# Top-k attention with a mixture of experts: split up products in the tail, small work and idle transposes elsewhere in the first steps

## The chip, the core and the metric

The kernel runs on one core of one Trainium2 chip. The engines are TensorE (PE in the profile; PEld its weight loads), VectorE (DVE), ScalarE (ACT), GpSimd (POOL) and SyncE (SP, which here issues DMAs). The metric is the device time of one execution in microseconds; less is better. "Clock" is TensorE's granted clock as a share of 2.4 GHz, so 0.50 is 1.2 GHz.

## What is computed

```python
# q, k, v: (8, 8, 576, 64); top_k = 32; 4608 tokens, D = 512, 8 experts, F = 1024
scores = scale * np.matmul(q, k.transpose(0, 1, 3, 2))
kth = np.partition(scores, -top_k, axis=-1)[..., -top_k:-top_k + 1]
scores = np.where(scores >= kth, scores, -1000000000.0)
attn = np.exp(scores - scores.max(-1, keepdims=True))
attn = attn / (attn.sum(-1, keepdims=True) + 1e-09)
x = (attn @ v).transpose(0, 2, 1, 3).reshape(B * S, H * D)
logits = x @ w_gate
e_idx = np.argmax(logits, axis=1)
...
for e in range(E):
    mask = e_idx == e
    h = np.maximum(x[mask] @ w1[e], 0.0)
    out[mask] = gate_w[mask, None] * eom[mask, e, None] * (h @ w2[e])
```

## The kernel before, in words

Rows of queries come in 36 tiles of 128; a step handles two heads of one tile, so there are 144 steps (`NSTEP`), and four steps make a tile. In step i DVE finds the largest scores of step i in three rounds (`rank`: L308 MAX, L311 MATCH_REPLACE), ACT then marks what lies below the 24th (`below`, L335), POOL adds marks and scores (L338), DVE takes the next eight from that sum (`window`, L350), reads the scores of the step after (`gmax`, L301), picks the 32nd value of step i-1 (`choose`: L361 twice, in the first steps also L365) and multiplies that step's exponentials by the mask (`weigh`, L377). In the first steps, i < `LONE` = 48 and not `exact`, called `calm`, the second head is masked on another way: `choose` leaves the negated value (L365), ACT marks with it (`veil`, L384), POOL adds (L387), and ACT takes the exponential (`unveil`, L393). PE computes scores (L274), transposes the weighted exponentials (`flip`, L404), and on even steps multiplies by v (`attend`, L436). On odd calm steps, where there is no `attend`, it transposes the identity 12 times into a bank that nobody reads (the idle transposes, L910).

What is done per finished tile and per group of tiles (sums and reciprocals L501 and L502, gates, routing L520 to L566, tables of slots) waits in queues and is issued one operation at a time by `fill(n)`. Its calls stood between the rounds of `rank` (three of one), before and after `choose` (one each) and at the end of the step (three). PE's part of it (`side_start`, "side work") goes beside the transposes of a step.

Tokens are routed in groups; each group gives expert slots of 128 tokens with one expert each, 40 in all. A slot loads w1 and w2 of its expert (2 MB each, L670 and L677 on SP's queue), gathers its rows (`fetch_x`, POOL), transposes them (`turn`), multiplies by w1 (`up_products`, L714, 128x128 pieces in plain f32), rectifies, multiplies by w2 (`down`) and scatters (`put`, L740). 25 slots are done inside the steps. The other 15, called the tail and numbered 25 to 39 here, follow after the last step in `slots_in_turn`: there w2 is split into two factors of type f32r, a rounded part (ACT, L1015) and the rest (DVE, L1016), the rectified result likewise (L1023, L1024), and the down product is three products of 128x512 for each of eight pieces (L1033). Buffers: two each of w1t and w2t, so a load waits until the readers of the buffer two slots back are done. Each engine takes its instructions in the order in which the program issues them. The table of the last slots (`slot_table(..., True)`, 25 small DVE operations) is issued by `background` during the first tail slot.

Of the kernel before, what the change touches and what calls it, by code (L numbers as in the profile page):

```python
# [23 lines left out]
P = 128  # L24
# [15 lines left out]
def tile_topk_attention_moe(  # L40
# [143 lines left out]
    def run(exact, stack):  # L184
# [688 lines left out]
        for i in range(NSTEP + 4):  # L873
            t, hp = divmod(i, NHP)
            step[0] = i
            if i + 1 < NSTEP and (i + 1, 0) not in SC:
                scores(i + 1)()
            for r in range(3):
                if i < NSTEP:
                    rank(i, r)  # L880
                    if r == 0:
                        shift(i)
                fill(1)
# [6 lines left out]


            calm = i < LONE and not exact
            mid = None
# [52 lines left out]
            fill(1)  # L946
            if 1 <= i <= NSTEP:
                choose(i - 1)
                fill(1)
# [8 lines left out]
            fill(3)  # L958
# [40 lines left out]
        def slots_in_turn():  # L999

            def prepare(n):
                ahead("id", fetch_id, n + 2)
                ahead("x", fetch_x, n + 1)
                ahead("w1", fetch_w1, n)
                ahead("w2", fetch_w2, n)

            def turned(n):
                ahead("turn", lambda s, *_: turn(s, pools["p"], "pm")(), min(n, had["x"] - cur[0]))

            def split(s, part):  # L1010

                w = W[s][1][:, 4 * part:4 * part + 4]
                hi, lo = [pools["w"].tile([P, 4, DM], F32R, name=n, bufs=3) for n in ("w2h", "w2l")]
                HL[s, part] = hi, lo
                nc.scalar.activation(hi, w, AF.Copy)  # L1015
                nc.vector.tensor_tensor(lo, w, hi.bitcast(F32), op=ALU.subtract)  # L1016

            def up_split(s, f0):
                if f0 == 0:
                    HT[s] = [pools["w"].tile([P, NF, P], F32R, name=n, bufs=1) for n in ("hth", "htl")]  # L1020
# [5 lines left out]
            def down_split(s, f0):  # L1026
                if f0 == 0:
                    PY[s] = pools["p"].tile([P, DM], F32, name="pm")
                hh, hl = HT[s]
                wh, wl = HL.pop((s, f0 // 4))  # L1030
                for f in range(f0, f0 + 4):
                    for k, (h, w) in enumerate(((hh, wh), (hh, wl), (hl, wh))):
                        nc.tensor.matmul(PY[s], h[:, f, :], w[:, f - f0, :], start=(f == 0 and k == 0),  # L1033
                                         stop=(f == NF - 1 and k == 2))

            def splitted(s, part):
                if s < min(len(order), had["w2"]) and (s, part) not in HL:
                    split(s, part)
            while cur[0] < len(order):
                s = cur[0]  # L1040
                prepare(1)
                turned(1)
                prepare(2)
                splitted(s, 0)
                splitted(s, 1)
                ahead("w2", fetch_w2, 3)
                for f0 in (0, 4):
                    up_split(s, f0)
                    yield
                ahead("w1", fetch_w1, 3)  # L1050
                turned(2)
                for part in range(2):
                    splitted(s + 1, part)
                    down_split(s, 4 * part)
                    yield
                put(s)
                cur[0] += 1
# [8 lines left out]
        background()  # L1066
        for _ in slots_in_turn():
# [77 lines left out]
```

## Time and profile before

| | us |
|---|---|
| median of 3 runs (1290.36 to 1293.07) | 1291.58 |
| profiled execution, time | 1289.37 |
| profiled execution, span from first to last instruction | 1287.5 |
| PE busy | 1185.5 (92%) |
| DVE busy | 1136.0 (88%) |
| ACT busy | 981.1 (76%) |
| POOL busy | 755.9 (59%) |

Busy shares are means over stretches with different limits: the calm steps take up the first 340 us or so, the other steps run to about 1060 us, the tail from 1080 to 1276 us. What a change is worth is read in its own stretch. Durations of PE's records overlap, so the distance between starts is the better measure there.

### The profile page before, as it was taken

To read this page: it belongs to the slowest core of one execution; us is meant where nothing else is said; L and a number is where in the kernel's file an instruction comes from. 1 tells how busy PE (TensorE), PEld (TensorE's weight loads), DVE (VectorE), ACT (ScalarE), POOL (GpSimd) and SP (SyncE) were. 2 spreads that over 40 slices of the span, in tenths; PEclk is the share of its full clock that TensorE was granted. 3 is DMA by queue.
4 is the path that set the end of the run, shared out by engine and by line. 5 is a ranking of instruction groups with operands and counts; after the bars stand their busy time and mean duration, and the time that the engine had idled before them with its cause. 6 is when DMAs were issued, how large, how long until landed. Compare 5 with 4: busy or idle time off the path is not lost.

```text
span 1287.5 us, 31729 instructions
## 1 busy us (share of the span) xinstructions
PE 1185.5 (92%) x10084; PEld 918.3 (71%) x10084; DVE 1136.0 (88%) x6112; ACT 981.1 (76%) x1928; POOL 755.9 (59%) x1221
## 2 busy tenths in 40 slices
PE   6777777777799999999999999999999999999996
PEld 4554655655577777777777777777777777999995
DVE  7999999999999999999999999999999954544443
ACT  6999999899888888878888888888878854454542
POOL 6666666698775766756767666567656733212110
PEclk7989899899899999999999999999999999999998
DMA  5400210201827663765465565755554468999980
GB/s 136 76 17 18 71 54 18 55 18 55 295 79 228 208 224 107 252 226 157 171 202 162 203 220 151 273 208 182 181 173 149 165 228 295 386 366 337 364 336 21
DMA packets 109384, 227.49 MB, mean 177 GB/s; under 512 B 14858, under 2 KB 33546, under 8 KB 108176
## 3 DMA queue, kind: packets, MB, share of 16 engines
q1 hardware_dynamic: 99536, 205.67, 47.6%
q0 software_dynamic: 7552, 18.96, 4.3%
q8 instruction: 83, 1.36, 0.5%
q10 hardware_dynamic: 2112, 0.68, 0.3%
q14 instruction: 101, 0.83, 0.2%
HBM read 206.68 MB, written 20.69 MB: 177 GB/s over the span
## 4 chain that ended last, share of the span: by engine, by line
PE 57%; DVE 26%; issue 14%; POOL 3%; ACT 1%; POOLq 0%; ACTq 0%
PE pm L714 14%; PE pm L729 13%; PE po L436 9%; PE ps L274 9%; PE pst L404 8%; DVE cand L301 8%; DVE v L350 5%; DVE cand L311 3%; DVE ep L377 3%; DVE v L308 3%; DVE x L361 2%; PE pst L457 1%; POOL xg L693 1%; PE pst L703 1%; POOL out_dram L740 1%
## 5 line engine op out<-in xcount | busy, mean ns | idle before, releaser
L338 POOL TENSOR_TENSOR w<-s,marks 128x576 f32<-128x576 f32 x288 | 362.8, 1281 | 191.0 <-ACT marks L335 184.5
L301 DVE MAX8 cand<-s 128x8 f32<-128x72 f32 x2304 | 322.0, 218 | 8.0 <-ACT s L282 8.0
L714 PE MATMUL pm<-xs,w1t 128*128 128x128 f32 x2560 | 296.8, 276 | 0.9 <-ACT xs L706 0.8
L714 PEld LDWEIGHTS pm<-xs,w1t 128*128 128x128 f32 x2560 | 292.0, 192 | 2.4 <-ACT xs L706 1.1
L404 PE MATMUL pst<-ident,ep 128*128 128x128 f32 x1296 | 210.6, 291 | 66.0 <-ACT ep L393 60.9
L404 PEld LDWEIGHTS pst<-ident,ep 128*128 128x128 f32 x1296 | 152.0, 146 | 152.2 <-ACT ep L393 68.7
L335 ACT ACTIVATE marks<-s,v 128x576 int8<-128x576 f32 x288 | 220.8, 770 | 40.8 <-DVE v L308 38.9
L350 DVE MAX8 v<-w 128x8 f32<-128x576 f32 x288 | 202.2, 744 | 0.0
L412 ACT ACTIVATE pT<-pst 128x512 f32<-128x512 f32 (+1 forms) x432 | 197.9, 481 | 5.5 <-PE pst L404 4.2
L282 ACT ACTIVATE s<-ps 128x1152 f32<-128x1152 f32 (+1 forms) x145 | 162.5, 1121 | 50.0 <-PE ps L274 49.9
L274 PE MATMUL ps<-kst,qst 64*128 64x288 f32 (+1 forms) x1280 | 189.7, 448 | 5.4 <-ACT s L282 5.4
L377 DVE SCALAR_TENSOR_TENSOR ep<-s,kth,ep 128x576 f32<-128x576 f32 x240 | 188.4, 814 | 0.3 <-issue 0.3
L436 PE MATMUL po<-pT,v 128*64 128x128 f32 (+3 forms) x3200 | 188.6, 270 | 0.0
L436 PEld LDWEIGHTS po<-pT,v 128*64 128x64 f32 (+1 forms) x3200 | 160.6, 139 | 34.4 <-issue 32.8
L729 PE MATMUL pm<-w2t,ht 128*128 128x512 f32 x400 | 180.4, 594 | 0.0
L345 ACT ACTIVATE ep<-s,v 128x576 f32<-128x576 f32 x240 | 175.5, 778 | 0.0
L740 POOL DMA_INDIRECT out_dram<-y,idt x40 | 49.9, 1247 | 189.5 <-ACT y L736 173.2
L308 DVE MAX8 v<-cand 128x8 f32<-128x64 f32 x864 | 147.7, 213 | 0.0
L274 PEld LDWEIGHTS ps<-kst,qst 64*128 64x128 f32 (+1 forms) x1280 | 101.6, 184 | 46.2 <-issue 18.2
L729 PEld LDWEIGHTS pm<-w2t,ht 128*128 128x128 f32 x400 | 72.4, 191 | 72.3 <-issue 72.3
L311 DVE MATCH_REPLACE8 cand<-v,cand 128x64 f32<-128x64 f32 x576 | 116.1, 209 | 0.0
L1016 DVE TENSOR_TENSOR w2l<-w2t,w2h 128x2048 fp32r<-128x2048 f32 x30 | 67.9, 2290 | 29.8 <-ACT w2h L1015 29.8
(165 smaller groups left out, 1434.8 us busy)
## 6 DMA issues: line engine op xcount, KB each, us to landing
w1t<-in_w_dram SPq DMA_DIRECT2D x40, 2048.0 KB, 9.4
w2t<-in_w_dram SPq DMA_DIRECT2D x40, 2048.0 KB, 11.7
v<-in_va_dram SPq DMA_DIRECT2D x8, 1152.0 KB, 6.8
x_rows<-xu SPq DMA_DIRECT2D x36, 256.0 KB, 2.1
qst<-in_qa_dram SPq DMA_DIRECT2D x70, 128.0 KB, 10.8
kst<-in_ka_dram SPq DMA_DIRECT2D x14, 576.0 KB, 8.1
ids<-far SPq DMA_DIRECT2D x1, 678.0 KB, 10.8
xg<-x_rows,idt POOLq DMA_INDIRECT x40, 7.0
```

Of the source, the lines that this page charges most:

```text
L274: nc.tensor.matmul(ps[qs, a, n, :288], Q[t][rows, hp, qs], K[b][rows, hp, cols], start=True, stop=True)
L301: nc.vector.max(out=c[:, 8 * g:8 * g + 8], in_=SC[i, a][:, g * GW:(g + 1) * GW])
L308: nc.vector.max(out=vs[:, a, 8 * r:8 * r + 8], in_=cs[a])
L335: nc.scalar.activation(m.bitcast(I8).rearrange("p (s b) -> p s b", b=2)[:, :, 1], s, AF.Sign, bias=vs[:, a, PIVOT - 1:PIVOT], scale=-(1.0 ...
L338: nc.gpsimd.tensor_tensor(w, s, m, op=ALU.add)
L350: nc.vector.max(out=VV[i][0][:, a, 24:32], in_=SW[i][0][a])
L377: nc.vector.scalar_tensor_tensor(e, SC.pop((i, a)), kth_col(i, a), e, op0=ALU.is_ge, op1=ALU.mult, accum_out=SM[t][:, 2 * hp + a:2 * hp + ...
L404: nc.tensor.transpose(ps[:, c - c0, :], pt[:, c * P:(c + 1) * P], ident)
L412: nc.scalar.activation(x, ps[:, :n, :], AF.Copy)
L436: nc.tensor.matmul(po[a * 64:(a + 1) * 64, k, qs], lhs, rhs, start=half and not k and not m, stop=(c == 3 and k == 1 and m == len(TT[t]) - 1))
L714: nc.tensor.matmul(ph[:, f - f0, :], w[:, c, f * P:(f + 1) * P], XS[s][:, c, :], start=(c == 0), stop=(c == NC - 1))
L729: nc.tensor.matmul(PY[s], HT[s][:, f, :], w[:, f, :], start=(f == 0), stop=(f == NF - 1))
```

## The change

In calm steps `fill` is no longer called between the rounds of `rank` nor before `choose`; it issues up to four between `choose` and `weigh` and up to four at the end. On steps with neither `attend` nor side work beside the transposes, 24 idle transposes stand for 12. In the tail x and w1 are split as w2 was, the up product becomes 12 products of 128x512 for each half of F with x as the stationary side, and its rectified result, which now has tokens on partitions, is transposed by PE (`turn_half`) before it is split. The slots overlap: the down product of slot s-1 stands after the up product of slot s. The first tail slot keeps the plain up product (`up_plain`). The last table is issued before the first tail slot where nothing else is pending.

```diff
@@ the loop over steps
+            calm = i < LONE and not exact
             for r in range(3):
                 if i < NSTEP:
                     rank(i, r)
...
-                fill(1)
+                if not calm:
+                    fill(1)
...
-                for c in range(12):
+                for c in range(12 if beside else 24):
                     nc.tensor.transpose(idle[:, c % 4, :], ident, ident)
...
-            fill(1)
+            if not calm:
+                fill(1)
             if 1 <= i <= NSTEP:
                 choose(i - 1)
-                fill(1)
+                fill(4 if calm else 1)
                 weigh(i - 1)
...
-            fill(3)
+            fill(4 if calm else 3)
@@ slots_in_turn
+            def parted(x, hi, lo):
+                nc.scalar.activation(hi, x, AF.Copy)
+                nc.vector.tensor_tensor(lo, x, hi.bitcast(F32), op=ALU.subtract)
+            def splitted(s, m, half):
+                if s < min(len(order), had["w2" if m else "w1"]) and (s, m, half) not in HL:
+                    w = W[s][m][:, 4 * half:4 * half + 4] if m else W[s][m][:, :, 512 * half:512 * half + 512]
+                    HL[s, m, half] = parts([P, 4, 512], (("w1h", "w1l"), ("w2h", "w2l"))[m])
+                    parted(w, *HL[s, m, half])
+            def products(ps, x, c0, w, first, last):
+                for c in range(4):
+                    for k, (a, b) in enumerate(((0, 0), (0, 1), (1, 0))):
+                        nc.tensor.matmul(ps, x[a][:, c0 + c, :], w[b][:, c, :], start=(first and c == 0 and k == 0),
+                                         stop=(last and c == 3 and k == 2))
+            def up_half(s, half):
+                ph = pools["p"].tile([P, 512], F32, name="pm")
+                products(ph, XS[s], 0, HL.pop((s, 0, half)), True, True)
+                HS[half] = pools["w"].tile([P, 4, P], F32, name="hs")
+                nc.scalar.activation(HS[half].rearrange("p c q -> p (c q)"), ph, AF.Relu)
+            def turn_half(s, half):
...
+                for c in range(4):
+                    nc.tensor.transpose(pt[:, c, :], HS[half][:, c, :], ident)
+                parted(pt, *[x[:, 4 * half:4 * half + 4, :] for x in HT[s]])
...
+                    up_half(s, 0)
                     yield
+                    splitted(s + 1, 0, 0)
+                    up_half(s, 1)
+                    yield
+                    turned(2)
+                    splitted(s + 1, 0, 1)
+                if done is not None:
+                    down_half(done, 0)
+                    yield
+                if s is not None:
+                    splitted(s, 1, 0)
+                    turn_half(s, 0)
+                    turn_half(s, 1)
+                if done is not None:
+                    down_half(done, 1)
+                    put(done)
+                    yield
+                if s is not None:
+                    splitted(s, 1, 1)
@@ ahead of the tail
+        if not (urgent or small or side):
+            small_end()
+            small_end = None
+            background()
```

Three places in the order of instructions. The first is DVE in a calm step in which the sums of a finished tile are inverted (r is the reciprocal, v the values found, x the choice, ep the weighted exponentials); before:

```order
L377 SCALAR_TENSOR_TENSOR ep,sums<-s,kth,ep 128x576
L308 MAX v_1618<-cand 128x8 x2
L311 MATCH_REPLACE cand<-v_1618,cand 128x64 x2
L501 TENSOR_SCALAR r<-sums 128x8
L308 MAX v_1618<-cand 128x8 x2
L311 MATCH_REPLACE cand<-v_1618,cand 128x64 x2
L502 RECIPROCAL r<-r 128x8
L308 MAX v_1618<-cand 128x8 x2
```

and after:

```order
L350 MAX v_1571<-w 128x8 x2
L301 MAX cand<-s 128x8 x16
L361 SCALAR_TENSOR_TENSOR x_1803,kth<-left,n,v_1571 128x8
L361 SCALAR_TENSOR_TENSOR x_1805,kth<-left,n,v_1571 128x8
L365 TENSOR_SCALAR less<-kth 128x1
L501 TENSOR_SCALAR r<-sums 128x8
L502 RECIPROCAL r<-r 128x8
L377 SCALAR_TENSOR_TENSOR ep,sums<-s,kth,ep 128x576
```

L501 and L502 moved from the rounds of `rank`, behind the weighing, to between `choose` and the next weighing. The second is ACT at the start of the tail (y of slot 24, then x of slot 25); before:

```order
L736 ACTIVATE y<-pm,idt 128x512
L706 ACTIVATE xs<-pm 128x512
L1015 ACTIVATE w2h<-w2t 128x2048 x2
L1023 ACTIVATE hth<-pm 128x512 x2
L706 ACTIVATE xs<-pm 128x512
L1015 ACTIVATE w2h<-w2t 128x2048 x2
```

and after, where w1h and w2h are the rounded parts, hth and hs the rectified results of slots 25 and 26:

```order
L706 ACTIVATE xs<-pm 128x512
L1008 ACTIVATE w1h<-w1t 128x2048
L1066 ACTIVATE hth<-pm 128x512
L1008 ACTIVATE xsh<-pm 128x512
L1008 ACTIVATE w1h<-w1t 128x2048
L1066 ACTIVATE hth<-pm 128x512
L1008 ACTIVATE w2h<-w2t 128x2048 x2
L1045 ACTIVATE hs<-pm 128x512
L1008 ACTIVATE w1h<-w1t 128x2048
L1045 ACTIVATE hs<-pm 128x512
```

A split of w1 of slot 27 now stands on ACT between the two rectifying copies of slot 26. The third is PE in step 3, an odd calm step; before:

```order
L404 MATMUL pst<-ident,ep 128x128 x8
L910 MATMUL pm<-ident 128x128 x12
L404 MATMUL pst<-ident,ep 128x128
L274 MATMUL ps<-kst,qst 128x288 x4
```

and after:

```order
L404 MATMUL pst<-ident,ep 128x128 x8
L911 MATMUL pm<-ident 128x128 x24
L404 MATMUL pst<-ident,ep 128x128
L274 MATMUL ps<-kst,qst 128x288 x4
```

Only the number of idle transposes changed, here and on twelve more steps.

## Rows read from the trace of the kernel before

**Rows 1.** Stretches: length, busy time (count) by engine, clock, DMA share, GB/s.

```profile
core 0: us, PE busy (x) PEld busy (x) DVE busy (x) ACT busy (x) POOL busy (x), PEclk, DMA share, GB/s
0.00:340.00 340.00, 255.50 (x2319) 189.67 (x2319) 329.87 (x1984) 300.32 (x635) 234.66 (x346) 0.91 0.24 65
1080.00:1276.00 196.00, 195.58 (x1376) 180.86 (x1376) 95.03 (x94) 90.35 (x89) 36.88 (x43) 1.00 0.86 318
```

**Rows 2.** Timeline of calm steps: start, duration, engine, line, operation, [idle before, releaser].

```profile
105.57 0.81 DVE L377 SCALAR_TENSOR_TENSOR ep<-s,kth,ep 128x576 f32<-128x576 f32 x1
106.67 1.27 POOL L387 TENSOR_TENSOR w<-s,marks 128x576 f32<-128x576 f32 x1 [1.41 <-ACT marks L384]
106.97 1.01 DVE L501 TENSOR_SCALAR r<-sums 128x8 f32<-128x8 f32 x1
...
112.81 0.81 DVE L377 SCALAR_TENSOR_TENSOR ep<-s,kth,ep 128x576 f32<-128x576 f32 x1
...
119.05 0.81 DVE L377 SCALAR_TENSOR_TENSOR ep<-s,kth,ep 128x576 f32<-128x576 f32 x1
```

**Rows 3.** L501 to 340 us: group (busy us, mean ns), line (min/median/max ns).

```profile
L501 DVE TENSOR_SCALAR r<-sums 128x8 f32<-128x8 f32 x11 | 8.4, 760 | 0.0
...
L501 DVE TENSOR_SCALAR r<-sums x11: 160/1014/1077, 52.9 to 327.4; 128x8 f32<-128x8 f32 x11
```

**Rows 4.** Timeline of PE in two calm steps.

```profile
44.29 0.33 PE L404 MATMUL pst<-ident,ep 128*128 128x128 f32 x1 [2.37 <-ACT ep L393]
...
120.62 1.48 PE L910 MATMUL pm<-ident 128*128 128x128 f32 x12
124.94 0.47 PE L404 MATMUL pst<-ident,ep 128*128 128x128 f32 x1 [2.85 <-ACT ep L393]
```

**Rows 5.** Stretches right behind those two waits, columns as in rows 1.

```profile
44.00:48.00 4.00, 3.71 (x37) 2.71 (x39) 3.96 (x29) 3.62 (x8) 2.43 (x4) 1.00 0.86 297
125.00:128.00 3.00, 3.00 (x20) 1.45 (x21) 2.96 (x24) 1.90 (x4) 1.60 (x3) 0.50 0.00 0
```

**Rows 6.** Timeline of DVE, line L361 (`choose`) in calm steps.

```profile
77.63 1.01 DVE L361 SCALAR_TENSOR_TENSOR x<-left,n,v 128x8 f32<-128x8 f32 x1
78.56 0.22 DVE L361 SCALAR_TENSOR_TENSOR x<-left,n,v 128x8 f32<-128x8 f32 x1
...
131.69 0.91 DVE L361 SCALAR_TENSOR_TENSOR x<-left,n,v 128x8 f32<-128x8 f32 x1
...
213.37 0.97 DVE L361 SCALAR_TENSOR_TENSOR x<-left,n,v 128x8 f32<-128x8 f32 x1
```

**Rows 7.** Timeline of PE in the tail.

```profile
1093.58 7.30 PE L714 MATMUL pm<-xs,w1t 128*128 128x128 f32 x64
...
1100.72 0.60 PE L703 MATMUL pm<-ident,xg 128*128 128x128 f32 x4
1101.08 0.48 PE L1033 MATMUL pm<-w2h,hth 128*128 128x512 f32 x1
...
1237.39 7.31 PE L714 MATMUL pm<-xs,w1t 128*128 128x128 f32 x64
...
1250.46 7.31 PE L714 MATMUL pm<-xs,w1t 128*128 128x128 f32 x64
```

**Rows 8.** Groups in the tail (busy us, mean ns), and one row of ACT's timeline.

```profile
L1016 DVE TENSOR_TENSOR w2l<-w2t,w2h 128x2048 fp32r<-128x2048 f32 x30 | 67.9, 2290 | 29.8 <-ACT w2h L1015 29.8
L1015 ACT ACTIVATE w2h<-w2t 128x2048 fp32r<-128x2048 f32 x30 | 57.3, 1918 | 5.8 <-PE pm L1033 4.2 <-DMA w2t<-in_w_dram 1.6
...
1231.66 0.60 ACT L1023 ACTIVATE hth<-pm 128x512 fp32r<-128x512 f32 x1 [2.98 <-PE pm L714]
```

**Rows 9.** A stretch of the tail, columns as in rows 1.

```profile
1100.00:1120.00 20.00, 20.00 (x131) 18.04 (x131) 9.69 (x7) 10.97 (x11) 2.57 (x3) 1.00 1.04 392
```

**Rows 10.** Loads of w1t, slots 26 (first line) and 27: landing, issue on SP.

```profile
DMA to landing us min/median/max: 9.4/9.4/9.4
...
1087.86 0.37 SPq L670 DMA_DIRECT2D w1t<-in_w_dram  x1
...
DMA to landing us min/median/max: 15.1/15.1/15.1
```

More of the change, by code (lines that the diff above doesn't have):

```diff
@@ L889, in run @@
             early, late, last = [], [], []
-            calm = i < LONE and not exact
-            mid = None
+            mid, beside = None, None
             if calm and 2 <= i:
@@ L999, in slots_in_turn @@
         def slots_in_turn():
[L1001 to L1005, printed above, removed]
-            def turned(n):
[L1008 to L1016, printed above, removed]
@@ new lines, in turned @@
+            def turned(n):
+                ahead("turn", lambda s, *_: turn_split(s), min(n, had["x"] - cur[0]))
+                for s in range(cur[0], had["turn"]):
+                    if not isinstance(XS[s], list):
+                        x = XS[s]
+                        XS[s] = parts([P, NC, P], ("xsh", "xsl"))
+                        parted(x, *XS[s])
+            def splitted(s, m, half):
[3 more added lines that the diff above has]
+                    parted(w, *HL[s, m, half])
@@ L1019, in up_split, with up_plain @@
+            def up_plain(s, f0):
                 if f0 == 0:
-                    HT[s] = [pools["w"].tile([P, NF, P], F32R, name=n, bufs=1) for n in ("hth", "htl")]
+                    HT[s] = parts([P, NF, P], ("hth", "htl"))
                 ph = up_products(s, f0)
@@ L1024, in up_split @@
                 nc.vector.scalar_tensor_tensor(lo, ph, 0.0, hi.bitcast(F32), op0=ALU.max, op1=ALU.subtract)
[L1026 to L1048, printed above, removed]
-                    yield
[L1050 to L1054, printed above, removed]
-                    yield
-                put(s)
-                cur[0] += 1
+            if cur[0] == len(order):
+                return
@@ new lines, in slots_in_turn @@
+            done = cur[0]
+            ahead("id", fetch_id, 3)
+            ahead("w1", fetch_w1, 2)
+            ahead("w2", fetch_w2, 2)
+            if had["turn"] == done:
+                ahead("x", fetch_x, 2)
+                ahead("turn", lambda s, *_: turn(s, pools["p"], "pm")(), 1)
+            ahead("x", fetch_x, 3)
+            cur[0] += 1
+            for half in range(2):
+                splitted(done + 1, 0, half)
+                up_plain(done, 4 * half)
+                if not half:
+                    turned(1)
+                yield
@@ new lines, in slots_in_turn @@
+            ahead("w1", fetch_w1, 2)
+            splitted(done, 1, 0)
+            splitted(done, 1, 1)
+            while cur[0] < len(order) or done is not None:
+                s = cur[0] if cur[0] < len(order) else None
+                if s is not None:
+                    ahead("id", fetch_id, 3)
+                    ahead("x", fetch_x, 2)
+                    ahead("w1", fetch_w1, 1)
+                    ahead("w2", fetch_w2, 1)
+                    turned(1)
+                    for half in range(2):
+                        splitted(s, 0, half)
+                    ahead("w1", fetch_w1, 3)
+                    ahead("w2", fetch_w2, 2)
+                    ahead("id", fetch_id, 4)
+                    ahead("x", fetch_x, 3)
+                    up_half(s, 0)
+                    yield
+                    splitted(s + 1, 0, 0)
+                    up_half(s, 1)
+                    yield
+                    turned(2)
[11 more added lines that the diff above has]
+                    yield
+                if s is not None:
+                    splitted(s, 1, 1)
+                done = s
+                if s is not None:
+                    cur[0] += 1
```

18 lines of the change are left out of this document (17 added, 1 removed).

## The prediction

> **What bounds the kernel now.** I read the stretches first, then inside each the engine that never rests. The table of stretches [rows 1] shows two regimes. Over the first 340 us DVE is busy 329.87 us, while PE rests a quarter of the time at a mean clock of 0.91: these are the calm steps (i < LONE = 48, `exact` false), and DVE bounds them. From 1080 to 1276 us PE is busy 195.58 of 196.00 us while DVE and ACT are half idle: this is the tail, 15 expert slots, and PE bounds it. The middle (340 to 1060 us) keeps its code, since `calm` is false there.
>
> Inside the calm steps I take the time from one weighing (L377) to the next as the step's length, on DVE's and POOL's timeline [rows 2]. A plain step is 112.81 to 119.05 = 6.24 us. The step from 105.57 to 112.81 has 7.24: it holds L501, a 128x8 operation that took 1.01 us. L501 began at 106.97 and ended at 107.98, just after POOL's L387 (106.67 + 1.27 = 107.94). It waited for POOL inside its own duration. The groups by line and the line's own view [rows 3] say how often: 11 of them, 8.4 us, shortest 160 ns, median 1014.
>
> A second loss sits in the same steps. On PE's timeline [rows 4] the 12 idle transposes of L910 start at 120.62 and PE then waits 2.85 us for ACT, until 124.94. From 125 to 128 us the clock is 0.50, the 1.2 GHz level [rows 5]. One step later DVE's L361 takes about 1 us where its neighbour takes 0.22 [rows 6]; five steps show this, the first at 77.63, one at 131.69 (the drop just named) and the last at 213.37, each the step after such an odd step without side work. My reading: scores and transposes at half clock come late, ACT's marks with them, so POOL's L338 still runs when `choose` begins.
>
> In the tail I read PE's order and starts [rows 7]. Two slots follow each other at 1237.39 and 1250.46: 13.07 us. Of these the up products take 1100.72 - 1093.58 = 7.14, the four transposes of x 1101.08 - 1100.72 = 0.36, and the split down products the rest, 5.57.
>
> **The change part by part.** *Small work in calm steps.* Nothing is added or removed on DVE; L501 and L502 move from between the rounds of `rank` to between `choose` and the weighing. POOL's L387 starts 1.10 us after the weighing does (106.67 against 105.57) [rows 2], because ACT's `veil` copy lies between, so the two operations fall into a pause of POOL. Gain: 8.4 - 11 x 0.16 = 6.6 us [rows 3]. Behind them the weighing waits, some 0.35 us, still ahead of POOL's start; POOL then begins about 0.1 us later, and nobody waits on that. The routing groups that end in these steps (two, of some 17 operations each) now run four before the weighing and four after it, where POOL is busy again. An operation that meets L387 can wait its whole 1.27 us. I count two waits lost and two gained, so nothing, with 3 us to either side. The setup work on POOL in the first steps moves the same way; I take nothing for it.
>
> *More idle transposes.* On 13 odd steps without side work 24 stand where 12 stood. They add another 1.48 us on PE [rows 4], which there waits 2.85 us anyway, so the wait falls to about 1.4. A wait of 2.37 us [rows 4] left the clock at 1.00 [rows 5], so I expect four of the five drops to go: 4 x (0.97 - 0.22) = 3.0 us [rows 6]. Bounds: 0, if the clock falls all the same, and 3.8. If the cover were gone, the extra transposes would delay ACT's next copy by up to 1.5 us in 13 steps; at full clock they end well before ACT does.
>
> *Tail: factors of the up products split too.* Per slot 64 records of L714 (32 products of 128x128) go; 24 matmuls of 128x512 on the split pairs (w1h, xsh), (w1l, xsh), (w1h, xsl) come, plus eight 128x128 transposes of the rectified result. No row shows those 24, but they have the form of the down products, 5.57 us; the eight transposes cost twice 0.36 = 0.72. A slot then takes 5.57 + 0.36 + 5.57 + 0.72 = 12.22 us of PE against 13.07: 0.85 less, over 14 slots (the first keeps `up_plain`) 11.9 us.
>
> Who must keep up with 12.22 us? ACT: four splits at 1.918 (before: two) and seven 128x512 copies at 0.60, together 11.9 at most [rows 8]. DVE: four at 2.290, which is 9.2, and three 128x512 ones, some 11. DMA: 2 x 2.097 MB of weights and 2 x 0.262 MB of gather and scatter, 4.72 MB, which at the 392 GB/s of 1100 to 1120 us is 12.0 us [rows 9]. All four stand within 8% of each other, so I expect PE to lead, narrowly. The buffers of w1t and w2t come free after the splits instead of after the products, so loads start earlier in the slot.
>
> Three stalls take back most of it. First, the start. ACT's order puts the first split of w1 of the third tail slot (27) ahead of the second relu of slot 26. That load starts when `up_plain` is done, at 1087.86 in the trace [rows 10], and about 1088.2 after the change. The two bounds for its landing are the load before it, 9.4 us, and this load itself, 15.1 us with another queued just ahead of it [rows 10]. By 9.4 us ACT is done with split and relu at 1088.2 + 9.4 + 1.92 + 0.6 + 0.2 = 1100.3; PE has run out at 1087.9 + 5.57 + 0.36 + 2.79 = 1096.6 (`up_half` twice, the turn, half of slot 25's down). That is 3.7 us of idle PE, 9.4 by the other bound. I take 4.5, since w2 of slot 27, the load that was ahead, now comes later. Second, after such a wait the clock falls [rows 5]: some 3 us at half speed cost 1.5. Third, the end: ACT's copy of the last y but one (0.60), then split and rest of the last w2 half (1.92 + 2.29) make 4.8 us [rows 8], of which half a down product (2.79) hides all but 2.0. Tail: -11.9 + 4.5 + 1.5 + 2.0 = -3.9 us.
>
> *Last tables ahead.* The table's small DVE operations move from within the first tail slot to ahead of it, where DVE has nothing else; in the first slot they were hidden behind PE as well. Cost and gain nothing.
>
> **Sum:** -6.6 - 3.0 - 3.9 = -13.5 us. Against the profiled execution: span 1287.5 to 1274.0, its time 1289.37 to 1275.9. That execution lies 2.2 us below the median of the three runs, 1291.58; from the median the forecast is 1278.1.
>
> **The rivals.** *The loads hold the tail's pace.* Today's slot moves its 4.72 MB in 13.07 us, 361 GB/s. If that is all the memory gives, slots stay at 13.07, and 13 x 0.85 = 11 us come back: net -2.5, 1289.1. For it: a DMA share of 1.04, full, at 392 GB/s [rows 9], so little is left. Against it: those 392 GB/s over 20 us, and a share of 0.86 over the whole tail [rows 1]. The Trainium skill, "SBUF — State Buffer", Summary: rules for kernel authors, says to plan with about 358 GB/s between HBM and SBUF. By that an estimate is 13.2 us a slot and no gain at all; the row of 392 GB/s [rows 9] disagrees, and the measurement decides.
>
> *ACT's order sets the slot (slower).* ACT is filled to within 0.3 us of a slot and takes its work in order: relu waits for PE, splits wait for loads. Today it waits 2.98 us for PE before a rectifying copy [rows 8]. If one such wait is left per slot, the slot becomes 11.9 + 2.98 = 14.9 us: 13 x 2.7 = 35 us more, net +21, 1313. It ends slower from 13.5 us per slot on, that is from a wait of 1.6 us. Against it: each relu's reader, the transposes, stands half a down product later in PE's order, so a late relu is absorbed.
>
> *The moved work meets POOL again.* If the pushed weighing, which reads two SBUF operands, now waits for L387, the calm steps gain nothing: net -3.9, 1287.7. L361, also with two operands, does wait [rows 6]; but the weighing would have to start 1.1 us later, and 0.35 is added.
>
> **How the numbers follow.** Forecast 0.68, loads 0.12, ACT 0.09, POOL again 0.11. 0.2%, 2.6 us, is about what a measurement of this kernel can tell from no change. Faster: 0.66 of the forecast, 0.06 of POOL, 0.04 of the loads = 0.76. Same: 0.06 of the loads, 0.04 of POOL, 0.02 of the forecast = 0.12. Slower: ACT 0.09, loads 0.02, POOL 0.01 = 0.12. Low end: best values (6.6, 3.8, routing waits 3, tail -11.9 + 2 + 2.0 = -7.9) give -21, 1270. High end: the loads' 1289 and a start by 15.1 us, 1290.
>
> **What would show it.** Right: L501 at 0.16 us throughout, and its step at about 6.6 us; no clock of 0.50 after about 30 us; in the tail 12.2 us from slot to slot, one PE gap of 4 to 5 us near the third slot and a gap near the end. Wrong: slots at 13 us with a DMA share of one; slots at 14 with ACT never idle on PE's waits; L377 or L361 above 1 us in the calm steps.

## The result and the profile after

The changed kernel takes 1277.34 us, the median of four runs (1275.61 to 1278.69), against 1290.97 for the kernel before, run beside it (1289.24 to 1293.07). The ratio is 0.9889 with a 95% interval of 0.9875 to 0.9903: some 14 us less, or 1.1%, well clear of the noise. The profiled execution took 1277.66 us, with a span of 1275.8.

| | before, us | after, us |
|---|---|---|
| span of the profiled execution | 1287.5 | 1275.8 |
| its time | 1289.37 | 1277.66 |
| PE busy | 1185.5 | 1179.8 |
| DVE busy | 1136.0 | 1197.4 |
| ACT busy | 981.1 | 1043.8 |
| last weighing (L377) of the last step | 1046.71 | 1041.00 |
| from there to the end of the span | 240.8 | 234.8 |

The two spans differ by 11.7 us: 5.7 in the steps and 6.0 in the tail. The medians differ by 13.6, since the profiled execution of before happened to lie 1.6 us below its median and that of after 0.3 above.

The stretches, with the columns of [rows 1]; the second is the tail from its first product to its last:

```profile
core 0: us, PE busy (x) PEld busy (x) DVE busy (x) ACT busy (x) POOL busy (x), PEclk, DMA share, GB/s
0.00:340.00 340.00, 261.73 (x2488) 196.74 (x2489) 327.68 (x2025) 305.37 (x648) 240.31 (x353) 0.97 0.26 72
1075.00:1264.00 189.00, 185.19 (x930) 154.41 (x928) 160.13 (x110) 153.76 (x145) 34.84 (x43) 1.00 0.89 330
```

The clock of the first 340 us rose from 0.91 to 0.97. In the tail PE still hardly rests, but DVE and ACT, half idle before, are now busy for more than 80% of it: the splits of x, w1 and the rectified result stand on these two.

**The calm steps.** Timeline of DVE and POOL in the step that answers [rows 2], then the group of [rows 3]:

```profile
103.38 0.81 DVE L377 SCALAR_TENSOR_TENSOR ep<-s,kth,ep 128x576 f32<-128x576 f32 x1
...
104.48 1.28 POOL L387 TENSOR_TENSOR w<-s,marks 128x576 f32<-128x576 f32 x1 [1.40 <-ACT marks L384]
...
109.62 0.16 DVE L501 TENSOR_SCALAR r<-sums 128x8 f32<-128x8 f32 x1
109.82 0.20 DVE L502 RECIPROCAL r<-r 128x8 f32<-128x8 f32 x1
109.94 0.77 DVE L377 SCALAR_TENSOR_TENSOR ep<-s,kth,ep 128x576 f32<-128x576 f32 x1
...
110.72 1.28 POOL L387 TENSOR_TENSOR w<-s,marks 128x576 f32<-128x576 f32 x1 [1.39 <-ACT marks L384]
...
L501 DVE TENSOR_SCALAR r<-sums x11: 160/161/163, 57.9 to 325.2; 128x8 f32<-128x8 f32 x11
```

L501 stands in POOL's pause between L338 and L387 and takes 0.16 us, all 11 times. The step has 109.94 - 103.38 = 6.56 us, where it had 7.24. And L387 begins 0.78 us after the weighing does, just as the weighing ends; none of the weighings of the calm steps is longer than 0.83 us.

The idle transposes, PE's timeline in the odd step that answers [rows 4], and the stretch around it (columns as above), which answers [rows 5]:

```profile
117.71 2.78 PE L911 MATMUL pm<-ident 128*128 128x128 f32 x24
122.03 0.33 PE L404 MATMUL pst<-ident,ep 128*128 128x128 f32 x1 [1.53 <-ACT ep L393]
...
117.00:125.00 8.00, 6.47 (x63) 4.94 (x61) 7.93 (x53) 7.18 (x15) 5.59 (x7) 1.00 0.01 3
```

PE waits 1.53 us where it waited 2.85, and the clock stays at 1.00. All five stalls of L361 that [rows 6] stand for are gone. Late in the calm steps others are left or new. These are the ones of the trace of before, DVE's timeline (L522, L559 and L562 are operations of the routing):

```profile
237.62 0.80 DVE L559 TENSOR_SCALAR den<-den 128x7 f32<-128x7 f32 x1
244.31 1.28 DVE L562 SCALAR_TENSOR_TENSOR ez<-ez,den 128x7 f32<-128x7 f32 x1
319.75 1.81 DVE L522 TENSOR_TENSOR oh<-oh,first 128x24 f32<-128x24 f32 x1
346.44 0.85 DVE L361 SCALAR_TENSOR_TENSOR x<-left,n,v 128x8 f32<-128x8 f32 x1
```

And these of the trace after, DVE and POOL, with the stretch ahead of the last stall:

```profile
229.37 1.28 POOL L387 TENSOR_TENSOR w<-s,marks 128x576 f32<-128x576 f32 x1 [1.93 <-ACT marks L384]
229.43 1.25 DVE L559 TENSOR_SCALAR den<-den 128x7 f32<-128x7 f32 x1
...
237.24 1.28 POOL L387 TENSOR_TENSOR w<-s,marks 128x576 f32<-128x576 f32 x1 [1.26 <-ACT marks L384]
237.26 1.28 DVE L562 SCALAR_TENSOR_TENSOR ez<-ez,den 128x7 f32<-128x7 f32 x1
...
285.40 1.08 POOL L570 DMA_INDIRECT ids<-entry,posi  x1 [0.17 <-issue]
286.52 1.29 POOL L387 TENSOR_TENSOR w<-s,marks 128x576 f32<-128x576 f32 x1
...
288.54 2.51 POOL L338 TENSOR_TENSOR w<-s,marks 128x576 f32<-128x576 f32 x2
289.48 1.59 DVE L361 SCALAR_TENSOR_TENSOR x<-left,n,v 128x8 f32<-128x8 f32 x1
...
339.66 1.17 DVE L361 SCALAR_TENSOR_TENSOR x<-left,n,v 128x8 f32<-128x8 f32 x1
...
332.00:340.00 8.00, 5.54 (x27) 3.40 (x28) 7.16 (x45) 6.98 (x16) 4.98 (x8) 0.50 1.04 375
```

Each of these tiny operations ends when POOL's 128x576 one does: 229.43 + 1.25 = 230.68 and 229.37 + 1.28 = 230.65; 289.48 + 1.59 = 291.07 and 288.54 + 2.51 = 291.05. So L559 waits longer than before, L562 as long, L522's 1.81 us is gone (0.18 now), and the stall of 289.48 is new. The last one, 1.17 us, had 0.85 in the same step of before; it follows a stretch at clock 0.50, the 1.2 GHz level. PE's last idle transposes start at 321.08: from step 48 on the kernel issues none.

The new stall goes back to POOL's own small operations. Four of a slot table, which `fill` now issues between `choose` and `weigh`, start on POOL at 283.51, a scatter (L570) follows them, and L387 begins at 286.52, 1.86 us after ACT's marks for it were done at 284.66. L338 then comes late too, and L361 waits for it.

**The tail.** PE's timeline, answering [rows 7], in the order of the program:

```profile
1074.70 3.84 PE L714 MATMUL pm<-xs,w1t 128*128 128x128 f32 x32 [0.83 <-issue]
...
1094.10 0.66 PE L1052 MATMUL pst<-ident,hs 128*128 128x128 f32 x4 [2.42 <-ACT hs L1045]
...
1115.05 0.60 PE L1015 MATMUL pm<-ident,xg 128*128 128x128 f32 x4
...
1127.29 0.60 PE L1015 MATMUL pm<-ident,xg 128*128 128x128 f32 x4
...
1237.44 0.60 PE L1015 MATMUL pm<-ident,xg 128*128 128x128 f32 x4
...
1256.90 0.50 PE L1036 MATMUL pm<-w2l,hth 128*128 128x512 f32 x1 [0.48 <-DVE w2l L1009]
1261.10 0.50 PE L1036 MATMUL pm<-w2l,hth 128*128 128x512 f32 x1 [0.81 <-DVE w2l L1009]
```

From 1115.05 to 1237.44 ten slots pass, 12.24 us each, where [rows 7] show 13.07. PE waits at three places only: 2.42 us at the third slot and 1.29 at the end (0.83 ahead of the first product, as before). ACT's timeline at the gap, and ACT's and DVE's groups, answering [rows 8] and [rows 10]:

```profile
1091.65 1.91 ACT L1008 ACTIVATE w1h<-w1t 128x2048 fp32r<-128x2048 f32 x1 [4.38 <-DMA w1t<-in_w_dram]
1093.47 0.58 ACT L1045 ACTIVATE hs<-pm 128x512 f32<-128x512 f32 x1
...
L1009 DVE TENSOR_TENSOR w2l<-w2t,w2h 128x2048 fp32r<-128x2048 f32 x30 | 68.5, 2288 | 12.8 <-ACT w2h L1008 12.8
L1008 ACT ACTIVATE w1h<-w1t 128x2048 fp32r<-128x2048 f32 x28 | 53.7, 1918 | 5.7 <-DMA w1t<-in_w_dram 5.7
L1045 ACT ACTIVATE hs<-pm 128x512 f32<-128x512 f32 x28 | 16.8, 599 | 9.3 <-PE pm L1036 9.3
```

The rectifying copy that the transposes need stood behind a split that waited 4.38 us for its load. The stretch behind the gap, and one of the steady tail, which answers [rows 9]:

```profile
1094.00:1098.00 4.00, 3.90 (x19) 3.31 (x20) 4.00 (x3) 4.00 (x4) 0.00 (x0) 1.00 1.03 399
...
1140.00:1160.00 20.00, 20.00 (x101) 16.73 (x100) 18.32 (x13) 17.48 (x18) 2.40 (x4) 1.00 1.02 388
```

The clock did not fall behind the gap. In the steady tail PE is full, the DMA share is one, and DVE and ACT are at 90%: every resource stands close to its end there, and from this row alone nobody could say which sets the pace.

### The profile page after: what moved, and what is told of

The parts are those of the page before. It is cut to its first block, busy times and chain, and to the rows that moved or that the text cites. A ratio compares the mean times of both kernels' runs of the same rounds, so it can differ in the third digit from the quotient of the medians.

```text
span 1275.8 us, 31308 instructions
## 1 busy us (share of the span) xinstructions
PE 1179.8 (92%) x9792; PEld 898.1 (70%) x9792; DVE 1197.4 (94%) x6154; ACT 1043.8 (82%) x1984; POOL 755.4 (59%) x1221
## 5 line engine op out<-in xcount | busy, mean ns | idle before, releaser
L338 POOL TENSOR_TENSOR w<-s,marks 128x576 f32<-128x576 f32 x288 | 362.9, 1281 | 181.7 <-ACT marks L335 171.2
L404 PE MATMUL pst<-ident,ep 128*128 128x128 f32 x1296 | 207.0, 284 | 55.1 <-ACT ep L393 47.1
L404 PEld LDWEIGHTS pst<-ident,ep 128*128 128x128 f32 x1296 | 145.9, 142 | 142.5 <-ACT ep L393 57.8
L714 PE MATMUL pm<-xs,w1t 128*128 128x128 f32 x1664 | 194.7, 275 | 0.9 <-issue 0.8
L714 PEld LDWEIGHTS pm<-xs,w1t 128*128 128x128 f32 x1664 | 189.9, 192 | 1.4 <-issue 1.1
L377 DVE SCALAR_TENSOR_TENSOR ep<-s,kth,ep 128x576 f32<-128x576 f32 x240 | 188.0, 812 | 0.3 <-issue 0.3
L274 PE MATMUL ps<-kst,qst 64*128 64x288 f32 (+1 forms) x1280 | 181.4, 432 | 5.4 <-ACT s L282 5.4
L436 PE MATMUL po<-pT,v 128*64 128x128 f32 (+3 forms) x3200 | 185.1, 266 | 0.0
L436 PEld LDWEIGHTS po<-pT,v 128*64 128x64 f32 (+1 forms) x3200 | 157.8, 136 | 33.0 <-issue 31.3
L740 POOL DMA_INDIRECT out_dram<-y,idt x40 | 45.4, 1136 | 184.6 <-ACT y L736 167.3
L274 PEld LDWEIGHTS ps<-kst,qst 64*128 64x128 f32 (+1 forms) x1280 | 98.2, 178 | 44.6 <-issue 16.2
L387 POOL TENSOR_TENSOR w<-s,marks 128x576 f32<-128x576 f32 x48 | 61.5, 1280 | 52.7 <-ACT marks L384 52.4
```

The lines of the kernel that those rows point to most:

```text
L274: nc.tensor.matmul(ps[qs, a, n, :288], Q[t][rows, hp, qs], K[b][rows, hp, cols], start=True, stop=True)
L338: nc.gpsimd.tensor_tensor(w, s, m, op=ALU.add)
L377: nc.vector.scalar_tensor_tensor(e, SC.pop((i, a)), kth_col(i, a), e, op0=ALU.is_ge, op1=ALU.mult, accum_out=SM[t][:, 2 * hp + a:2 * hp + ...
L404: nc.tensor.transpose(ps[:, c - c0, :], pt[:, c * P:(c + 1) * P], ident)
L436: nc.tensor.matmul(po[a * 64:(a + 1) * 64, k, qs], lhs, rhs, start=half and not k and not m, stop=(c == 3 and k == 1 and m == len(TT[t]) - 1))
L714: nc.tensor.matmul(ph[:, f - f0, :], w[:, c, f * P:(f + 1) * P], XS[s][:, c, :], start=(c == 0), stop=(c == NC - 1))
```

## The experiments

Microseconds below are what the measured ratio to the kernel before takes off 1291 us, unless medians are named.

**The parts alone.** The first has the `fill` lines of the diff, the second the line of the idle transposes, the third the new `slots_in_turn` with the last tables:

```diff
@@ first
-                fill(1)
+                fill(4 if calm else 1)
...
@@ second
-                for c in range(12):
+                for c in range(12 if beside else 24):
@@ third
-            def split(s, part):
+            def parted(x, hi, lo):
...
```

> The kernel before with the move of the small work in the calm steps alone: 12 idle transposes, old tail. Theory A (each part acts by itself; the two traces are read step by step): L501 falls to 0.16 us in all 11 steps, which saves about 4.5 us net up to the step at 228 us, and the routing steps after it give 1 to 4 us back, since their operations at the step's end meet L387; the stalls of L361 near 1 us after odd steps stay (five of them). So 1 to 5 us faster than before, about 2.5, with the clock over the first 340 us still near 0.91. Theory B (the stalls of L361 went because of the fill's move, not because of the transposes): 5 to 7 us faster, L361 at 0.22 in the steps at 77 to 213 us.

> The kernel before with 24 idle transposes for 12 alone. Theory A: L361 at 0.22 us in the five steps that showed about 1 us (77 to 213 us), clock of the first 340 us at about 0.97, 3 to 3.8 us faster; L501 keeps its 1 us. Theory B: the five stalls stay or come elsewhere, within 1 us of the time before, though the clock is higher.

> The kernel before with the new tail alone (with the last tables ahead of it). Theory A: the parts add up; the tail is worth what the two traces show, 6.0 us, 12.24 us from slot to slot and one gap of 2.4 us near the third slot, so 1285 us. Rival: the start of the tail depends on how the steps ended (which loads were issued when), then the gap is another, between 0 and 5 us, and the time 1282 to 1288. The three parts alone should come to the 13.6 us by which the changed kernel is faster; if they come to 2 us more or less, the parts meet each other.

The small work alone: 1288.13 us, ratio 0.9967 (0.9954 to 0.9979), 4.3 us. L501 is at 0.16 us in all 11 steps, the clock of the first 340 us at 0.91 as before, and L361 still stalls: in two of the five steps as before (1.00 us at 181.74 and 208.69), in a third for 0.59, and in others (1.00 at 266.80). It also has the new stall of the changed kernel, 1.59 us at 294.17. The idle transposes alone: 1288.16 us, 0.9974 (0.9963 to 0.9984), 3.4 us; clock 0.96, all five stalls of L361 are gone, and one of 0.77 came in another step, at 144.81, behind a stretch at 0.50. By the medians the two are 3.3 us each. In both theory A held in what it said of the time: each part mends its own stall. Not all five stalls stayed without the transposes, though. (Theory A of the first named the step at 228 us as the point from which routing takes back; it does, with L559 at 1.25 us.)

The new tail alone: 1289.45 us, 0.9986 (0.9975 to 0.9996), only 1.8 us, outside what either theory allowed. The sum of the three is 9.5 us where the whole gave 14.3, by the sign of the expectation the parts meet each other. Timeline of PE at the third slot, and the stretch behind it:

```profile
1099.89 1.09 PE L1050 MATMUL pst<-ident,hs 128*128 128x128 f32 x4 [2.94 <-ACT hs L1043]
...
1100.00:1104.00 4.00, 4.00 (x13) 3.32 (x14) 4.00 (x3) 4.00 (x4) 0.00 (x0) 0.58 1.03 386
```

The gap was 0.52 us longer than in the changed kernel, and behind it the clock was low until about 1103: products start 0.43 us apart (1101.21, 1101.63) where they start 0.23 apart elsewhere. From first product to last this tail takes 1271.22 - 1080.00 = 191.22 us against 1263.81 - 1074.70 = 189.11. So 2.1 us more: 0.5 of it the gap, the other 1.6 about the cost of the clock.

**Steps together, and the new tail without its gap.** The first is the first two parts of above. The second is the tail alone with this edit, in the third slot only:

```diff
-                    splitted(s + 1, 0, 0)
                     up_half(s, 1)
                     yield
+                    splitted(s + 1, 0, 0)
```

> The kernel before with the moved small work and the 24 idle transposes together, old tail. Alone they gave 4.3 and 3.4 us by the medians. Theory A (they act in different steps and add): 6.5 to 8 us faster than before, 1283 to 1284.5, with L501 at 0.16 us and L361 at 0.22 up to about 280 us. Rival (they meet each other): below 5 us, or above 9, and then the traces must show in which steps.

> The steps of the kernel before (12 idle transposes, small work where it was) with the new tail, and in it the second rectifying copy of slot 26 ahead of the split of w1 of slot 27. The new tail alone gave only 1.8 us; its trace shows a wait for hs of 2.94 us with the clock at 0.50 behind it, and a last scatter that landed about 1.9 us later than in the other runs. Theory A (the gap and the clock loss behind it are what the tail alone lacked): the gap falls to about 0.7 us, the clock stays at 1.00 from 1090 to 1120 us, and the time is 3 to 4.5 us below that of the new tail alone, near 1285.5. Rival (the missing microseconds lie in the steps or in the scatter): 1.5 to 2.4 us from the gap alone, 1287 to 1288.

The steps together: 1283.57 us, 0.9938 (0.9925 to 0.9951), 8.0 us against 4.3 + 3.4 = 7.7 alone (7.3 against 6.6 by the medians): they add. The tail without its gap: 1285.43 us, 0.9953 (0.9941 to 0.9964), 6.1 us, 4.3 more than with it, a time as theory A had it. Its trace has no wait for hs, two of 0.71 and 1.34 us for the next up product, and a clock of 1.00 from 1100 to 1120. So the gap and the clock behind it are a part of what the tail alone lacked, but not all is placed: the two traces show 1.8 us of the 4.3 between first and last product (189.45 against 191.22). The edit did not take the whole gap there, since its load was slower (10.50 us against 9.56, see below). Where the rest of the 4.3 lies is open. It would be in executions that were not profiled; the profiled one is the fastest of the tail alone and the slowest of the other.

**The gap in the changed kernel, and the order of ACT.** The same edit on the changed kernel, in the third slot only and in every slot:

> The changed kernel, but in the third tail slot (27) the first split of w1 stands on ACT behind the second rectifying copy of slot 26 instead of ahead of it. Theory A (the gap of 2.42 us at the third slot is ACT's order, as the prediction had it): no wait of PE for hs there; the next one is the up product of slot 27 itself, whose split still ends some 4 us after the load, so a wait for DVE's w1l of 0 to 1 us; 1.5 to 2.4 us faster than the changed kernel, and the clock stays at 1.00. Rival (the load itself is the limit): the gap only moves behind the down products of slot 25, 2 us or more, and the time stays within 0.5 us.

> The changed kernel with the second rectifying copy ahead of the first split of the next slot's w1 in every slot. Theory A (ACT has slack of 1.5 us a slot, the order matters only at the start): 12.24 us from slot to slot as before. Rival (ACT then waits for PE's up product in every slot, with the split behind it, and the split comes late for the next up product): slots of 12.6 to 14 us.

In the third slot: 1275.04 us, 0.9878 (0.9861 to 0.9896), 2.3 us by the medians below the changed kernel, though the intervals overlap. PE's wait there is now another and shorter one:

```profile
1093.19 0.50 PE L1036 MATMUL pm<-w1l,xsh 128*128 128x512 f32 x1 [0.69 <-DVE w1l L1009]
```

From the last weighing to the end this trace has 1271.6 - 1038.43 = 233.2 us against 234.8: 1.6 less, close to 2.42 - 0.69 = 1.7. In every slot (one run, 1277.58): 12.24 us from slot to slot all the same. ACT's order has slack in the steady tail; the rival that ACT's order sets the slot falls.

At the third slot the edit of every slot is the same as the first, yet two waits are left there, 0.71 and 1.34 us. The traces tell why: the load of w1 for that slot took longer. From its issue on SP to ACT's first use of it, us, and PE's waits at the third slot:

| | load to first use | waits of PE |
|---|---|---|
| all small work ahead of the weighing (below) | 8.59 | 1.97 |
| changed kernel | 9.07 | 2.42 |
| tail alone | 9.56 | 2.94 |
| copy first in the third slot | 8.86 | 0.69 |
| both (below) | 8.85 | 0.64 |
| copy first in the third slot, tail alone | 10.50 | 2.05 |
| copy first in every slot | 10.51 | 2.05 |

In the first three the wait is the load less 6.6 us, in the others the load less 8.2 to 8.5. So the order of ACT costs 1.6 to 1.8 us of the gap, as theory A had it, and the load sets the rest, as the rival had it. The tail alone had the longer gap because its load took 0.5 us longer. Why the loads differ stays open.

**What comes after PE.** One of three products left out in the tail:

```diff
-                    for k, (a, b) in enumerate(((0, 0), (0, 1), (1, 0))):
+                    for k, (a, b) in enumerate(((0, 0), (0, 1))):
```

> The changed kernel with two of the three products of each pair in the tail (the product of the remainder of the left side with the rounded weights is left out, so the output is less exact). It frees PE of 16 of 48 products of 128x512, some 3.6 us of a 12.24 us slot, and leaves loads, splits and copies as they are: what then sets the slot is the next limit. Theory A (loads are next, 4.72 MB at 380 to 395 GB/s): 11.9 to 12.3 us from slot to slot with a DMA share of one, so almost no gain. Rival (ACT and DVE next, ACT at 10.6 us of work a slot): 10.6 to 11.5 us a slot. Second rival (PE alone counts): 8.6 us a slot, 50 us faster.

One run, 1264.26 us. The transposes of x stand at 1112.50 and, ten slots on, at 1223.79: 11.13 us each, 10.3 to 10.6 in the first three and up to 11.7 later. Stretches of its tail:

```profile
1140.00:1160.00 20.00, 16.01 (x77) 12.00 (x76) 19.34 (x14) 18.43 (x20) 9.87 (x6) 1.00 1.04 394
...
1180.00:1200.00 20.00, 15.98 (x75) 11.93 (x75) 18.00 (x11) 17.22 (x17) 7.71 (x5) 1.00 1.04 398
```

PE falls to 16 of 20 us and the slots get shorter, so it was PE that set 12.24. But 3.6 us fewer products gave 1.1 us: loads, DVE and ACT stand right behind. In the later slots ACT waits for loads of w2t (6.2 us from 1180 to 1240): 4.72 MB at 398 GB/s is 11.9 us, near the 11.5 to 11.7 seen there. From 1112 to 1150 it waits 0.2 us for loads; DVE and ACT are at 97% and 92% from 1140 to 1160. So both theories seem to hold half, the first slots by DVE and ACT, the later ones by the memory; no run takes these apart. A DMA share of one stood in both tails; it alone did not tell that loads were the limit.

**The last tables.** Issued in the first tail slot again:

```diff
-        if not (urgent or small or side):
-            small_end()
-            small_end = None
-            background()
```

> The changed kernel without the issue of the last tables ahead of the tail: their 25 small operations stand in the first tail slot again. The prediction took nothing for this. Theory A: within 1 us of the changed kernel (1277.3 us). Rival (they stand ahead of the remainders of the split w1 on DVE, which PE waits for at the second slot): a new wait of PE for w1l of 1 to 3 us near 1080 to 1090 us, and as much slower.

1277.80 us, 0.9903 (0.9888 to 0.9917): 0.5 us above the changed kernel by the medians, with overlapping intervals. The gap moved, though. PE's timeline and two stretches:

```profile
1088.74 0.50 PE L1036 MATMUL pm<-w2l,hth 128*128 128x512 f32 x1 [2.57 <-DVE w2l L1009]
...
1088.00:1092.00 4.00, 3.26 (x9) 2.54 (x10) 4.00 (x3) 4.00 (x5) 0.00 (x0) 0.71 1.02 405
1092.00:1096.00 4.00, 4.00 (x21) 3.31 (x20) 4.00 (x4) 3.82 (x4) 0.00 (x0) 0.87 0.94 313
```

The small operations stand ahead of the splits on DVE, PE now waits 2.57 us for w2l instead of 2.42 for hs, and the clock falls. Its trace has 1274.6 - 1038.48 = 236.1 us from the last weighing to the end, 1.3 more than the changed kernel. So the tables ahead are worth about one microsecond by the traces; the intervals of the times do not tell it from nothing.

**Edits that go on from there.** All eight calls ahead of the weighing in calm steps; then that with the edit of the third slot; then both with the products in another order:

```diff
-                fill(4 if calm else 1)
+                fill(8 if calm else 1)
...
-            fill(4 if calm else 3)
+            fill(0 if calm else 3)
```

```diff
-                for c in range(4):
-                    for k, (a, b) in enumerate(((0, 0), (0, 1), (1, 0))):
+                for k, (a, b) in enumerate(((0, 0), (1, 0), (0, 1))):
+                    for c in range(4):
```

> The changed kernel with all eight calls of the small work between choice and weighing and none at the end of a calm step. Theory A (what the calm steps gave back, 1.3 us in the routing steps at 220 to 236 us, came from operations at the step's end that met L387): L559 and L562 at their short times there, 1 to 2.5 us faster than the changed kernel. Rival: up to eight operations of 0.16 us delay the weighing by up to 1.3 us, it starts after POOL's L387 has begun and waits for it: weighings above 1.5 us, 0 to 3 us slower. A third reading, that the stalls of L361 near 290 and 340 us come from POOL's own small operations, is not touched by this run: they stay.

> The two edits of the last two runs together, on the changed kernel. If both theories hold, 3 to 4.5 us faster than the changed kernel, 1273 to 1274.5 us; if the two places are independent, the difference is the sum of the two others within 1 us.

> The two edits on the changed kernel that gave 1271.4 us together (all small work ahead of the weighing, the rectifying copy first in the third slot), and the products of each half in another order: the four with both rounded parts first, then the four with the remainder of the left side, then the four with the remainder of the weights, which DVE makes last. Theory A (PE's waits for w2l at the end, 0.5 and 0.8 us, and for w1l at the third slot, 0.6, are DVE's 2.3 us behind ACT's split): eight products, 1.9 us, now cover them; these waits go, 1.5 to 2 us faster, 1269.5 to 1270. Rival (ACT's split of w2h is as late as DVE's remainder): the wait comes back under w2h, no more than 0.5 us faster.

All ahead of the weighing: 1271.94 us, 0.9860 (0.9839 to 0.9881), 5.4 below the changed kernel by the medians and 3.7 by the ratios; more than theory A's 1 to 2.5. (One of its five runs took 1276.73, the others 1271.3 to 1272.1.) L559 and L562 are at 0.16 us. DVE and POOL:

```profile
233.96 0.16 DVE L559 TENSOR_SCALAR den<-den 128x7 f32<-128x7 f32 x1
...
235.10 1.28 POOL L387 TENSOR_TENSOR w<-s,marks 128x576 f32<-128x576 f32 x1 [1.66 <-ACT marks L384]
```

The three routing steps take 7.97 + 6.72 + 7.22 = 21.91 us against 24.73 in the changed kernel: 2.8. The stalls of L361 near 290 and 340 us went as well, which is another 1.4 us at the first of them, though others came (1.28 at 253.47, 0.55 to 0.80 from 299 to 335). The third reading had said that they stay. Its cause, POOL's small operations, is what the trace of the changed kernel shows at 289.48; but this edit moves those operations too. No weighing of the calm steps is longer than 0.82 us, so the rival fell.

Both edits: 1271.36 us, 0.9849 (0.9834 to 0.9865), 6.0 us below the changed kernel by the medians, more than was expected, but not the sum: the third slot's edit gave 0.6 by the medians on top of the other, 1.0 in the spans. With the other order of products: 1269.44 us, 0.9832 (0.9819 to 0.9844), another 1.9, a time as theory A had it. At the end PE's waits for w2l come to 0.2 us instead of 1.3; at the third slot the wait did not go, it is 0.73 for xsl now. From the last weighing to the end the two traces differ by 1.4 us. This version beats both kernels.

## Why the prediction was right, and where its terms were not

The forecast was 1278.1 us and the sum -13.5; measured are 1277.34 and -13.6 by the medians. The three mechanisms were as told, L501's wait for POOL, the clock behind PE's waits, and fewer microseconds of PE per slot. That the sum met the time to 0.1 us is luck: the terms were off in both directions and cancelled, the steps gave less, the tail more.

- **Small work, forecast -6.6, alone -4.3.** The stall of L501 went in full: 8.4 - 11 x 0.16 = 6.6 us of DVE's time, some 0.7 in each step that held a long one. "Two waits lost and two gained, so nothing" came out about right over both routing groups: the first lost 1.4 (its three steps grew from 7.78 + 7.33 + 8.22 = 23.33 to 24.73 us), the second gained 1.1 in steps 42 to 46, L501 left out. The run with nothing behind the weighing shows that 2.8 us more could be had in the first. What the sum had left out is POOL's own small work: the step with the stall at 289.48 grew from 6.25 to 7.62 us. The Trainium skill, "SBUF — State Buffer", Summary: rules for kernel authors, says that when a DVE operation with two inputs in SBUF and a GpSimd one that reads there meet, the second to issue is blocked until the first is done. The rows of L562 and L361 above, which end with POOL's operation to within 0.02 us, agree. L501 and L559 list a single input and wait just so.
- **Idle transposes, forecast -3.0, alone -3.4.** All five stalls went, and PE's wait fell to 1.53 us for the 1.4 of the forecast. But the reason that was given, that a wait of 2.37 us leaves the clock at 1.00, is no rule: the same trace also has the opposite, as the last section shows.
- **The two together** give 8.0 us by the times, against 9.6. In the trace the last weighing is only 5.7 us earlier. At step 31 it was 8.3 us ahead; the first routing group took 1.4 and the stall at 289.48 another 1.4, steps 41 to 46 gave 2.2 back, 1.1 of them L501's, and steps 47 to 60 took 2.0 again. The two losses of 1.4 are no chance. In all seven traces with these calls, the small work alone among them, the three routing steps take 23.6 to 24.7 us (22.6 to 23.3 in the four with the old calls) and the step of the stall 7.6 (6.2 to 7.0). What does vary is in which of the earlier steps L361 stalls, not the same ones in the three traces with the old calls and 12 idle transposes, and the stretch from step 47 on. Six executions with both parts end their steps 5.6, 5.7, 6.0, 7.0, 8.2 and 8.3 us ahead of before, and two with the old steps 0.4 us ahead and 4.1 behind.
- **The tail, forecast -3.9, measured -6.0 in the trace.** The slot was 12.22 by the sum and is 12.24. The 24 products had no row, and the down products were the right price for them. PE leads, narrowly, as said. What was mis-sized are the three stalls, 8.0 us forecast and 3.7 measured. Start: 2.42 us for 4.5. The working gave 3.7 with the 9.4 us load of [rows 10] and 9.4 with the slower one, and 4.5 was chosen between them. The load was as fast as the faster: issued at 1082.58, its first use at 1091.65, 9.07 us, and in the other traces of the table 8.6 to 10.5. And PE held out until 1091.68, 9.1 us after that issue instead of 8.4; 0.36 of this are the first four transposes of hs, which had been left out. Clock: 0 for 1.5, but the term is real: it came in the tail alone (2.94 us of gap) and in the run without the tables ahead (2.57). End: 1.29 for 2.0. With 14 x 0.83 = 11.6 us gained these 3.7 leave 7.9; from first product to last the traces show 6.7 (195.81 against 189.11), and the end behind the last product is 0.7 longer (11.99 against 11.27), so 6.0. Of the 1.2 us between, 0.6 lie at the same three gaps: between the starts of PE's records they cost 2.7, 0.6 and 1.0, so 4.3. No single wait holds the other 0.6.
- **Tables ahead, forecast 0.** About 1 us of gain by the traces: PE did not cover them in the first slot, since DVE's splits stood behind them.
- **The signs.** L501 at 0.16 and slots of 12.2 us came as told; the clock did not stay up (0.50 behind the stall at 289.48, from 294 to 296 us, and from 332 to 340).
- **The rivals.** Loads: refuted at 12.24, but they stand 5% behind. [rows 9] already had 392 GB/s, and the run with two products reached 398. ACT's order: refuted; its waits for PE sum to 9.3 us over 28 copies, and moving the copies in every slot did not change the slot. POOL again: for the weighing refuted, true for L559, L562 and the L361 at 289.48.

## What to carry to other kernels

When parts of a change act in different stretches, run each alone and all together: a sum that comes out right may hide terms that cancel, and a part that seems to be worth little (here the tail, 1.8 us) may carry a gap that one moved copy removes. When a small operation is long beside a neighbour's large one and ends with it, try it in the neighbour's pause: here all eight calls there beat four ahead and four behind by 5.4 us by the medians. Look at what else the calls move: four of POOL's own operations in that pause made it late for its next large one. If several engines stand within 10% of one another, take work from the one in front before you promise a gain: 3.6 us less of PE gave 1.1.

## What the runs showed of the hardware

A gap of PE can cost its length and the clock behind it. In the tail the clock stayed at 1.00 after a wait of 2.42 us and fell to 0.50 after waits of 2.57 and 2.94; the longer gap of the tail alone cost 2.1 us more, 0.5 of it the gap. But the length of the wait alone does not tell. [Rows 4, 5] have a wait of 2.37 us with 1.00 behind it and one of 2.85 with 0.50; the same trace also has one of 2.85 with 1.00 behind it and one of 2.37 with 0.62. PE's timeline and the stretches there:

```profile
98.35 0.33 PE L404 MATMUL pst<-ident,ep 128*128 128x128 f32 x1 [2.85 <-ACT ep L393]
332.16 0.33 PE L404 MATMUL pst<-ident,ep 128*128 128x128 f32 x1 [2.37 <-ACT ep L393]
...
100.00:104.00 4.00, 3.40 (x48) 2.75 (x46) 4.00 (x26) 4.00 (x9) 3.41 (x5) 1.00 0.19 67
332.00:336.00 4.00, 3.84 (x21) 2.41 (x21) 3.93 (x33) 3.35 (x7) 3.51 (x5) 0.62 1.03 419
```

What else decides it, no run here shows.

The end of the span lies 10 to 13 us behind the issue of the last scatter, and not always the same. POOL's last row of the changed kernel (span 1275.8) and of the tail alone (span 1285.1):

```profile
1264.89 0.98 POOL L740 DMA_INDIRECT out_dram<-y,idt  x1 [6.64 <-ACT y L736]
```

```profile
1272.29 0.98 POOL L740 DMA_INDIRECT out_dram<-y,idt  x1 [6.64 <-ACT y L736]
```

That is 10.9 us and 12.8, with 10.2 before. The DMA share falls to 0.00 in the windows from 1271 and from 1279 us, 6 to 7 us after the issue; what fills the rest, and why the whole varies by 2 us, stays open.

This kernel on one core drew 388 to 398 GB/s over stretches of 20 us in the tail with 2 MB loads. The Trainium skill, "HBM Reference", Specifications (TRN2), gives about 425 for a core that streams alone and 358 where both cores of a pair do; the rows lie between the two.
